# Two edits around the start of the second layer: where the first batch's last filter sums lie, and the order of the weights' sums on GpSimd

## The chip, the cores and the metric

The kernel runs on one core of a Trainium2 chip. The metric is the device time of one execution in microseconds (us). Lower is better. The engines are called as in the profile: PE (TensorE) does matmuls and PEld is its weight load; DVE is VectorE, ACT is ScalarE, POOL is GpSimd and SP is SyncE, which here only issues DMAs. Each engine takes its instructions strictly in the order in which the program emits them for it; a "queue" below is this order.

## The reference

A batch of 8 sequences (3008 positions, 256 channels) is filtered along the positions in the Fourier domain, and the result goes through a two-layer network with a hard-swish between the layers.

```python
X = np.fft.rfft(x, axis=1)                      # x: (8, 3008, 256)
Y = X * (filt_r + 1j * filt_i)[None]            # (1505, 256) filters
y = np.fft.irfft(Y, n=3008, axis=1).reshape(24064, 256)
h = y @ moe_w_in                                # (256, 2048)
g = h * np.clip(h + 3.0, 0.0, 6.0) / 6.0
out = g @ moe_w_out                             # (2048, 256)
```

## The kernel before

The Fourier transform is done by matmuls with tables, since 3008 is 47 times 64: a first stage (`a_unit`, or `a0_unit` for batch 0), a second (`b_unit`), the product with the filter (`f_unit` makes products, `y_unit` the sums of products, lines 454 to 461), and two inverse stages (`bi_unit`, `n_unit`) with trips through DRAM between them (`z_tmp`, `g_tmp`). For batch 0 all of this runs first, in the first 67 us; the batches 1 to 7 are threaded into the network's steps.

The network runs over 47 blocks of 512 tokens and, in each, over 8 pairs `p` of 128 hidden columns (256 columns a pair), so there are 8 steps to a block. Block 0 is done plainly (`plain_up`, `plain_down`: four products of 128 by 512 each way). From block 1 on, which is step 8, a Strassen-like scheme with seven products replaces eight (`up_1` to `up_5`, `g_sums`, `down`). It needs sums of weights beside the weights. The tile `w_all` has, for each pair and each of the two matrices, seven slots of 128 columns; the slots 0 to 3 take the raw weights and are read by the plain steps. `w_sums(i, late)` makes the sums for matrix `i % 2` of pair `i // 2` on GpSimd: with `late` false, three sums into the slots 4, 5 and 6, which read slots 0 to 3; with `late` true, one sum that overwrites slot 1, and so has to come after the plain step of that pair. That is 8 operations a pair, 64 in all. `up_1` of a pair needs the slot 0 and then slot 4 (`S1`) of its input matrix.

The weights come as 64-bit floats and are converted on DVE: `w_conv(i)`, seven instructions (lines 275 to 293) that turn the loaded words into slots 0 to 3 of a matrix; a pair is two conversions. The conversions 0 to 3 are done during batch 0, the other twelve in the steps 0 to 6 by `convert_one`: one in step 0, two in each of the steps 1 to 5, and number 15, the last, in step 6. A conversion's last instruction is at line 293. The load of the words of conversion `i + 2` goes out on SP's queue when the buffer of `i` is free.

The order is written out by hand: `plan` holds what is to be emitted at each step, and `at(step, fn, ...)` appends to it. In a plain step the order is `plain_up(p)`, then the step's early units (matmul stages, among them `bi_unit`), then `plain_down(p - 1)`, then the rest in the order of the `at` calls (conversions, sums of weights, stores, loads). Inside `plain_up`, `relu(i)` (line 615, ACT) reads the matmul's result from PSUM into a buffer `r`, and `hswish` (line 620, DVE) multiplies, and frees the PSUM tile.

Buffers come from rotating pools: a new tile takes the place of the oldest of its tag and waits for that one's readers. The tag `r` of the pool `rp` has two; it is used by a zero tile at the start, by the `y` tiles of batch 0, and by every `relu`. The pool `t1p` has two buffers of the tag `t1`; in batch 0 they take the results of `bi_unit(0, 0)`, `(0, 4)` and `(0, 8)`, which `g_store` writes to DRAM from GpSimd's queue, and afterwards the first stage's results of the later batches. The `y` tiles that matter here are those of `y_unit(0, 10)` and `y_unit(0, 11)`: they are read by `direct` (line 545) and, in step 0, by `bi_unit(0, 10)` (line 471).

`t_sums(k)` (line 563), four differences of the tokens of block `k`, is also on GpSimd's queue, between sums of weights.

Of the kernel before, what the change touches and what calls it, by code (L numbers as in the profile page):

```python
# [10 lines left out]
FP32 = mybir.dt.float32  # L11
# [20 lines left out]
P = 128  # L32
D = 256
# [12 lines left out]
NP = DFF // 256  # L46
# [90 lines left out]
def kernel(  # L137
# [25 lines left out]
    def pool(name, bufs, **kw):  # L163
        return ctx.enter_context(tc.tile_pool(name=name, bufs=bufs, **kw))

    const = pool("const", 1)
    t1p = pool("t1p", 2)
    t2p = pool("t2p", TB)
    sp = pool("sp", 2)
    yp = pool("yp", 3)  # L170
    t3p = pool("t3p", T3B)
    xtp = pool("xtp", 2)
    rp = pool("rp", 2)
# [21 lines left out]
    st = {}  # L195
# [257 lines left out]

    def y_unit(b, i):
        s1, s2 = st["y", b, i]
        y = yp.tile([P, 2, D], FP32, name="y") if b else rp.tile([P, 512], FP32, name="r", tag="r").rearrange(
            "p (u d) -> p u d", u=2)
        re, im = slice(0, HALF), slice(HALF, P)
        nc.vector.tensor_tensor(out=y[re], in0=s1[re], in1=s1[im], op=ALU.subtract)
        nc.vector.tensor_tensor(out=y[im], in0=s2[re], in1=s2[im], op=ALU.add)  # L460
        st["y", b, i] = y
# [271 lines left out]
    def at(step, fn, *a):  # L733
        plan.setdefault((step, fn in EARLY), []).append((fn, a))

    with tc.manual_schedule():
# [66 lines left out]
        for c in range(NT):  # L803
            for i in (2 * c, 2 * c + 1):
                b_unit(0, i)
                f_unit(0, i)
                if c == NT - 1:
                    y_unit(0, i)
            if c + 1 < NT:
                turn(c + 1)  # L810
            if c:
                bi_unit(0, 2 * c - 2)
                (g0_first if c == NT - 1 else lambda i: g_store(0, i))(2 * c - 2)
            if c == 4:
                t4_load(0, 0, KH - 3 * TC, 1)
# [22 lines left out]

        for i, s in enumerate((0, 1, 1, 2, 2, 3, 3, 4, 4, 5, 5, 6)):
            at(s, convert_one)  # L840
        for p in range(NP):
            for i in range(2):
                for late in range(2):
                    at(p + 6, w_sums, 2 * p + i, late)

        at(0, wai_load)
        at(2, x_load, 1, 2)
# [42 lines left out]
        for n in range(1, B):  # L890
            a_at, f_at, y_at, bi_at = places(n)
            for c, s in enumerate(a_at):
                at(s, a_unit, n, c)
                if n > 1:
                    at(s, a_sums, n, c)
                at(s, z_store, n, c, nc.sync if n == 1 else nc.gpsimd)
                if c >= 3:
                    at(max(a_at[c - 3], s - 6), x_load, n, c)
                elif n > 1:
                    at(max(prev[c + NB - 3], s - 6), x_load, n, c)  # L900
            for c in range(NT):
                s = f_at[2 * (c - TB) + (n == 1)] + 1 if c >= TB else a_at[-1] + 1
                at(s, t2_load, n, c)
                s = f_at[2 * (c - FB) + 1] + 1 if c >= FB else a_at[-1 if n > 1 else 3] + 1
                at(s, table_load, n, c)
            for i in range(NU):
                if i % 2 == 0 or n == 1:
                    at(f_at[i], b_unit, n, i)
                if i % 2 == 0:
                    at(bi_at[i // 2], bi_unit, n, i)  # L910
                    at(bi_at[i // 2], g_store, n, i)
                at(y_at[i], y_unit, n, i)
            for i in range(NU):
                at(f_at[i], f_unit, n, i)
            prev = a_at
# [4 lines left out]
        for i in range(len(items) + 1):  # L920
            up = i < len(items)
            k, p = items[min(i, len(items) - 1)]
# [92 lines left out]
```

## Time and profile before

| | |
|---|---|
| time, median of 6 runs | 2708.59 us (2706.83 to 2712.05) |
| the profiled execution: its own time | 2708.02 us |
| its span, first to last instruction | 2706.2 us |
| mean granted TensorE clock | 0.998 of full speed |
| PE, DVE, ACT, POOL busy | 2676.8, 2023.9, 1307.9, 373.4 us |
| `plain_up` of pairs 0 to 7: PE begins at | 67.13, 73.39, 80.39, 88.49, 98.40, 109.30, 120.72, 132.17 us |
| step 8 (`up_1` of block 1, pair 0): PE begins at | 142.08 us |
| sums of weights on POOL | 40 from 106.33 us, 24 from 173.21 us |

The times inside the execution count from the start of the span. A timeline line gives the start, the length, engine and line, the operation, output and inputs with their shapes and the count; in brackets stands the idle time of the engine before it and what ended that. Several instructions of one kind are merged into one line. A window line gives, for each engine, its busy time and the number of its instructions in that stretch, then the granted clock of PE, the busy share of the DMA engines and GB/s.

### The profile page before, as it was taken

The numbers are of one execution on the slowest core, as the hardware profiler recorded it, in microseconds if no ns is written. First come the engines' busy times: TensorE is split into PE (matmuls) and PEld (weight loads), VectorE is DVE, ScalarE is ACT, GpSimd is POOL, SyncE is SP. The second block draws the span as 40 slices with busy tenths as digits, with TensorE's granted clock in tenths as the row PEclk, the third lists the DMA queues.
The fourth block names the chain that finished last, engine by engine and source line by source line (L and its number), as shares of the span: only waits on it lengthen the run. The fifth ranks groups of instructions, "written<-read, shape, count | busy, mean of one in ns | idle before, by whom it ended". The sixth has DMA issues, their size and how long they took to land.

```text
span 2706.2 us, 48891 instructions
## 1 busy us (share of the span) xinstructions
PE 2676.8 (99%) x18846; PEld 2366.4 (87%) x18846; DVE 2023.9 (75%) x3503; ACT 1307.9 (48%) x2614; POOL 373.4 (14%) x598
## 2 busy tenths in 40 slices
PE   9899999999999999999999999999999999999998
PEld 6588888888988889888888888988888888899997
DVE  7958867787678876777767877678776778766665
ACT  3344444444544544444444545445454454444443
POOL 2421111100120011200121011210112111000000
PEclk9999999999999999999999999999999999999999
DMA  8732123211232113321133111331113311110000
GB/s 240 205 100 68 49 81 103 73 32 44 80 106 71 35 40 90 104 63 35 46 97 97 55 38 50 92 96 55 38 54 89 96 58 36 42 31 17 18 9 17
DMA packets 106598, 185.89 MB, mean 69 GB/s; under 512 B 23609, under 2 KB 66297, under 8 KB 106049
## 3 DMA queue, kind: packets, MB, share of 16 engines
q1 hardware_dynamic: 88607, 138.05, 18.2%
q0 software_dynamic: 17152, 44.22, 6.2%
q8 instruction: 149, 2.44, 0.4%
q14 instruction: 84, 0.69, 0.1%
q10 hardware_dynamic: 606, 0.49, 0.1%
HBM read 110.74 MB, written 71.93 MB: 67 GB/s over the span
## 4 chain that ended last, share of the span: by engine, by line
PE 95%; DVE 2%; DMA 1%; SPq 0%; issue 0%; ACT 0%; POOL 0%; POOLq 0%; DVEq 0%
PE po L646 43%; PE al L570 24%; PE be L570 17%; PE psn L524 4%; PE psf L471 2%; PE psf L385 2%; PE psf L428 1%; PE po L352 1%; PE po L437 0%; DMA xs<-in_x_dram 0%; PE psf L437 0%; DVE g L620 0%; PE al L779 0%; DVE y L277 0%; DVE y L288 0%
## 5 line engine op out<-in xcount | busy, mean ns | idle before, releaser
L646 PEld LDWEIGHTS po<-w_all,g 128*128 128x128 f32 x10304 | 1363.1, 191 | 149.5 <-issue 41.4
L646 PE MATMUL po<-w_all,g 128*128 128x128 f32 x10304 | 1403.3, 276 | 0.6 <-DVE g L620 0.6
L615 ACT ACTIVATE r<-h,half_c 128x512 f32<-128x512 f32 x736 | 531.3, 722 | 329.4 <-DVE h L596 317.4
L620 DVE SCALAR_TENSOR_TENSOR g<-r,h 128x512 f32<-128x512 f32 x736 | 507.6, 690 | 206.6 <-ACT r L615 192.2
L570 PE MATMUL al<-xt,w_all 128*128 128x256 f32 x2208 | 660.1, 381 | 1.1 <-DVE h L601 0.6
L570 PE MATMUL be<-xn,w_all 128*128 128x256 f32 x1472 | 437.8, 379 | 0.0
L596 DVE TENSOR_TENSOR h<-be,s 128x512 f32<-128x512 f32 x368 | 254.3, 691 | 222.0 <-PE be L570 209.9
L570 PEld LDWEIGHTS al<-xt,w_all 128*128 128x128 f32 x2208 | 335.3, 192 | 2.5 <-issue 1.3
L570 PEld LDWEIGHTS be<-xn,w_all 128*128 128x128 f32 x1472 | 279.7, 190 | 37.9
L610 ACT ACTIVATE h<-al 128x256 f32<-128x256 f32 x368 | 141.4, 384 | 343.2 <-PE al L570 343.2
L601 DVE TENSOR_TENSOR h<-al,s 128x256 f32<-128x256 f32 x368 | 156.2, 425 | 166.0 <-PE al L570 164.8
L628 DVE TENSOR_TENSOR g<-g 128x512 f32<-128x512 f32 x368 | 255.9, 695 | 12.7
L591 ACT ACTIVATE s<-al 128x256 f32<-128x256 f32 x368 | 141.4, 384 | 205.4 <-PE al L570 203.3
L582 ACT ACTIVATE s<-be 128x256 f32<-128x256 f32 x368 | 141.4, 384 | 176.3 <-PE be L570 176.3
L570 PE MATMUL al<-xn,w_all 128*128 128x256 f32 x736 | 219.9, 381 | 0.5 <-ACT h L610 0.5
L570 PE MATMUL be<-xt,w_all 128*128 128x256 f32 x736 | 218.9, 379 | 0.0
L630 DVE TENSOR_TENSOR g<-g 128x256 f32<-128x256 f32 x368 | 169.9, 462 | 12.5
L581 ACT ACTIVATE s<-al 128x256 f32<-128x256 f32 x368 | 141.4, 384 | 70.9 <-PE al L570 70.8
L627 DVE TENSOR_TENSOR g<-g 128x256 f32<-128x256 f32 x368 | 157.0, 427 | 12.6
L570 PEld LDWEIGHTS be<-xt,w_all 128*128 128x128 f32 x736 | 139.8, 190 | 18.9
L402 POOL DMA_DIRECT2D z_tmp<-t x192 | 95.2, 502 | 417.5 <-DVE t L395 399.1
L563 POOL TENSOR_TENSOR xt<-xn 128x256 f32<-128x256 f32 x92 | 68.7, 747 | 473.8 <-ACT xn L530 453.5
(139 smaller groups left out, 1810.4 us busy)
## 6 DMA issues: line engine op xcount, KB each, us to landing
g_tmp<-t POOLq DMA_DIRECT2D x96, 256.0 KB, 3.7
t<-g_tmp SPq DMA_DIRECT2D x188, 120.0 KB
t<-z_tmp SPq DMA_DIRECT2D x42, 512.0 KB
z_tmp<-t POOLq DMA_DIRECT2D x192, 96.0 KB, 3.4
out_dram<-o SPq DMA_DIRECT2D x321, 47.0 KB
xs<-in_x_dram SPq DMA_DIRECT2D x112, 128.0 KB
ft<-in_filt_r_dram SPq DMA_DIRECT2D x168, 64.0 KB
ft<-in_filt_i_dram SPq DMA_DIRECT2D x168, 64.0 KB
```

What stands on the lines that cost most here:

```text
L570: nc.tensor.matmul(ps, w_in[p][:, w, :], x, start=start, stop=stop, skip_group_check=True)
L581: nc.scalar.activation(out=s[:, 0, :], in_=al, func=AXT.Copy)
L582: nc.scalar.activation(out=s5, in_=be[:, 1, :], func=AXT.Copy)
L591: nc.scalar.activation(out=s[:, 1, :], in_=al, func=AXT.Copy)
L596: nc.vector.tensor_tensor(out=st["h"][0].rearrange("p (a n) -> p a n", a=2), in0=be, in1=s, op=ALU.add)
L601: nc.vector.tensor_tensor(out=st["h"][1][:, 256:512], in0=al, in1=s5, op=ALU.add)
L615: nc.scalar.activation(out=r, in_=st["h"][i], func=AXT.Relu, bias=half_c, scale=1.0 / 6.0)
L620: nc.vector.scalar_tensor_tensor(out=st["g", k, p][:, o:o + 2, :].rearrange("p a n -> p (a n)"), in0=st["r", i], scalar=1.0, in1=st["h"][i ...
L627: v.tensor_tensor(out=g[:, G1, :], in0=g[:, G3, :], in1=g[:, G22, :], op=ALU.add)
L628: v.tensor_tensor(out=g[:, G3:G2 + 1:2, :], in0=g[:, G3:G1 + 1, :], in1=g[:, G11:G11 + 1, :].broadcast_to([P, 2, 256]), op=ALU.subtract)
L630: v.tensor_tensor(out=g[:, G4, :], in0=g[:, G12, :], in1=g[:, G2, :], op=ALU.subtract)
L646: nc.tensor.matmul(st["po", k][bank][:, part, u, :], g[:, a, ts(u, P)], w_out[p][:, w, :], start=(p == 0 and n in OPENS and u == 0), stop= ...
```

## The change

In the first hunk, the two `y` tiles of batch 0 take the two halves of one `t1` buffer instead of two `r` buffers. `y_unit(0, 10)` takes the buffer that `bi_unit(0, 0)` had, and `bi_unit(0, 8)`, which comes right behind, now takes the one that `bi_unit(0, 4)` had, not that of `bi_unit(0, 0)`.

In the second hunk, the six sums of pair 7 that don't overwrite raw weights (`w_sums(14)` and `w_sums(15)` with `late` false) go from step 13 to step 6, ahead of the sums of pair 0. The two late sums of pair 7 stay in step 13. The order on GpSimd's queue from step 6 on is then: six of pair 7, eight each of the pairs 0 to 4, `t_sums(2)`, eight each of the pairs 5 and 6, two of pair 7. Before it was eight each of the pairs 0 to 4, `t_sums(2)`, eight each of the pairs 5 to 7. The six sums read what the conversions 14 and 15 write.

```diff
     def y_unit(b, i):
         s1, s2 = st["y", b, i]
-        y = yp.tile([P, 2, D], FP32, name="y") if b else rp.tile([P, 512], FP32, name="r", tag="r").rearrange(
-            "p (u d) -> p u d", u=2)
+        if b == 0 and i % 2 == 0:
+            st["y0"] = t1p.tile([P, 2, 2, D], FP32, name="t1")
+        y = yp.tile([P, 2, D], FP32, name="y") if b else st["y0"][:, i % 2, :, :]
...
         for i, s in enumerate((0, 1, 1, 2, 2, 3, 3, 4, 4, 5, 5, 6)):
             at(s, convert_one)
+
+        for i in range(2):
+            at(6, w_sums, 2 * NP - 2 + i, False)
         for p in range(NP):
             for i in range(2):
-                for late in range(2):
-                    at(p + 6, w_sums, 2 * p + i, late)
+                if p < NP - 1:
+                    at(p + 6, w_sums, 2 * p + i, False)
+                at(p + 6, w_sums, 2 * p + i, True)
```

## The prediction

> **What bounds the kernel now.** I read the page first (engines, then the chain that ended last), then the timelines of PE, ACT, DVE and POOL from 66 to 190 us, where the edited lines run, and last the granted clock in small windows.
>
> ```profile
> PE 2676.8 (99%) x18846; PEld 2366.4 (87%) x18846; DVE 2023.9 (75%) x3503; ACT 1307.9 (48%) x2614; POOL 373.4 (14%) x598
> PE 95%; DVE 2%; DMA 1%; SPq 0%; issue 0%; ACT 0%; POOL 0%; POOLq 0%; DVEq 0%
> ```
>
> PE bounds the whole: its waits between 140 and 420 us, batch 1's stages included, are 1.6 us in all. A gain must come out of the 29 us in which PE is idle or out of matmuls that run slow, and what PE saves before 142 us lasts to the end, since all that follows is paced by PE. The waits that PE's timeline shows in the plain steps:
>
> ```profile
> 70.77 1.09 PE L471 MATMUL psf<-r,wi 64*64 64x512 f32 x8
> 73.39 1.98 PE L657 MATMUL al<-xn,w_all 128*128 128x512 f32 x4 [1.54 <-DVE g L620]
> ...
> 109.30 1.98 PE L657 MATMUL al<-xn,w_all 128*128 128x512 f32 x4 [0.82 <-DVE g L620]
> 120.72 1.98 PE L657 MATMUL al<-xn,w_all 128*128 128x512 f32 x4 [3.04 <-DVE g L620]
> 122.54 1.88 PE L657 MATMUL be<-xn,w_all 128*128 128x512 f32 x4
> 132.17 3.24 PE L657 MATMUL al<-xn,w_all 128*128 128x512 f32 x4 [3.08 <-DVE g L620]
> 135.20 2.36 PE L657 MATMUL be<-xn,w_all 128*128 128x512 f32 x4
> ```
>
> Four waits for DVE's hard-swish, 8.5 us, and after the last of them the same four matmuls take 3.24 instead of 1.98 us. The window of the granted clock (first value after the POOL count) says why:
>
> ```profile
> 133.00:134.00 1.00, 1.00 (x2) 0.34 (x1) 0.93 (x3) 0.00 (x0) 0.92 (x2) 0.50 0.80 168
> ```
>
> Half speed, from about 132.7 to 136.6 us. What DVE does before those waits, in a conversion at 89 us and in one at 115 us, and POOL:
>
> ```profile
> 89.24 0.75 DVE L277 SCALAR_TENSOR_TENSOR y<-bits,top_c,y 128x512 int32<-128x512 int32 x1
> 90.02 0.43 DVE L279 TENSOR_SCALAR y<-y 128x512 int32<-128x512 int32 x1
> 90.37 0.42 DVE L281 TENSOR_SCALAR bits<-bits 128x512 int32<-128x512 int32 x1
> ...
> 115.46 0.83 DVE L277 SCALAR_TENSOR_TENSOR y<-bits,top_c,y 128x512 int32<-128x512 int32 x1
> 116.32 0.56 DVE L279 TENSOR_SCALAR y<-y 128x512 int32<-128x512 int32 x1
> 116.81 0.68 DVE L281 TENSOR_SCALAR bits<-bits 128x512 int32<-128x512 int32 x1
> ```
>
> ```profile
> 106.33 28.48 POOL L299 TENSOR_TENSOR w_all<-w_all 128x128 f32<-128x128 f32 x40
> 169.96 0.73 POOL L563 TENSOR_TENSOR xt<-xn 128x256 f32<-128x256 f32 x1 [35.15 <-ACT xn L530]
> 173.21 14.38 POOL L299 TENSOR_TENSOR w_all<-w_all 128x128 f32<-128x128 f32 x24
> ```
>
> DVE has no idle time from 74 to 130 us and every conversion instruction is longer while POOL runs its 40 sums (106.33 to 134.81 us); at 135.14 us line 288 is back at 0.69 from 0.83. So in the plain steps 4 to 7 DVE is the bound, stretched by POOL's sums, which nobody needs before step 8.
>
> **First hunk: the buffer.** ACT's `relu` of pair 0 starts at 71.93 us after 4.14 us idle, put down to PE's line 471, `bi_unit(0, 10)`: that reads the `y` tiles, whose `r` buffers `relu` wants. With `y` elsewhere `relu` needs only its matmul. Pair 1 shows that latency: 73.39 to 75.42, so 67.13 + 2.03 = 69.16 us. The second: 75.22 to 77.13, so 68.95 + 1.91 = 70.86 us, and its hard-swish 0.74 later (72.52 to 73.26), 71.60 instead of 73.26. DVE is free of conversion 3 at 70.12 us, so conversion 4 starts 1.66 us earlier; its words landed by 66 us. PE goes on at 71.86 us, the end of line 471, instead of 73.39: 1.53 us.
>
> The added wait: `bi_unit(0, 8)` now writes the buffer of `bi_unit(0, 4)`, whose two stores left POOL at 45.5 and 46.0 us and took 5.6 and 6.1 us to land, so 52.1 us; ACT's copy (line 474) starts at 52.20. Behind it on ACT are the stores of `g0_first`, for which `t4_load`, `n_first` and pair 0 wait, so lateness is paid in full. Store landings of this line lie between 2.9 and 7.4 us, so the cost is 0 to 1.3; I take 0.2, by the row of this very store. `y_unit(0, 10)` itself waits for stores of 36 us, long landed. The two halves of one tile are tracked by region: at 153.77 us PE reads one slot of `g` while line 630 still writes another (to 154.3). Net: DVE 1.45 us earlier.
>
> **Second hunk: the order on POOL.** After `t_sums(1)` POOL now meets the sums of pair 7, which need conversion 14 (ends 131.51 us before) and 15 (137.35). So the stretch with the 40 sums beside the conversions 10 to 15 becomes idle. The time from one pair's first hard-swish on DVE to the next, with two conversions between, is 9.55 us without POOL (78.04 to 87.59), and was 11.10, 11.42 and 11.45 us for the steps that follow 97.47, 108.57 and 119.99. Saved: 1.87 and 1.90 in the last two; of the 1.55 in the first most is `t_sums(1)` (103.8 to 106.3), which stays: I take 0.45 (bounds 0.2 and 1.5). Sum 4.2 us. PE's own work per step is 8.37 us (109.30 to 117.67) against 9.55, so DVE stays the bound and the gain is PE's: with 1.45 before it, `plain_up` of pair 7 starts 5.7 us earlier, at 126.5 us, after waits of about 0.4, 1.1 and 1.2 us.
>
> Clock: the four matmuls each of `al` and `be` took 3.03 and 2.30 us to the next start against 1.82 and 1.81 in pair 6, so the drop cost 1.70 us. The drop followed the second idle time of 3 us in the trace (3.04, then 3.08); the new ones are at most 1.3. I count 1.70 as gained, bounds 0 and 1.70. [...]
>
> What becomes late: the sums of pair 0 are now behind conversion 15. It ends about 131.4 us; three sums of pair 7's output matrix, then S1, at 0.60 each (14.38 / 24, beside the network's DVE work) give 133.9 us. PE wants S1 at 142.51 - 5.7 - 1.7 = 135.1; at 126.5 us plus 3.6, 1.0 and 3.5 us of its own work and 0.43, the same. So no wait, with 1.2 us to spare. Pair by pair POOL needs 4.8 us and PE's steps are 7.0 to 8.4, so the slack grows; `t_sums(2)` comes at 163 us and POOL is through its 43 sums at about 157. Steps 8 to 11 get POOL's company on DVE: at 177 to 186 us it stretched lines 627, 628 and 630 by 0.14 each and PE had no gap there. I take 0.2 us for the switch at step 8. [...] The loads stay hidden: words come 3.9 to 5.0 us after their issue (at line 288 of two conversions before), and DVE then has 6.9 us of other work.
>
> **The sum.** 1.45 + 4.2 + 1.7 - 0.2 = 7.2 us off the profiled execution's 2708.02 (span 2706.2 plus 1.8 around it): 2700.8. The median of the runs stands 0.57 above that execution, so 2701.3.
>
> **Rivals.** (1) Partial gain: the clock still drops, or the new bound on DVE is a load (slack 1.9 to 2.3 us, with the same bytes in 5 us less), and 1.7 to 4 us of the 7.2 are lost: about 2704. For it: DMA engines are 0.8 to 0.9 busy in several windows there. Against: no DVE wait for words now. (2) The second hunk gives nothing, as the conversions are stretched by DMA traffic, not POOL: first hunk alone, 2708.6 - 1.4 = 2707. Against: the stretch ends with POOL's last sum at 134.8 while the DMA share stays at 0.8. (3) Slower: the sums of weights come late in block 1. In series from 131.5 us, S1 of pair 4 is the 36th sum; at d us each it is there at 131.5 + 36 d, and PE wants it at 175.92 - 7.4 = 168.5. Up to d = 1.03 nothing is paid; at 1.23 the whole 7.2 is gone, and at 1.4 the time is 2708.6 + 6 = 2715. For it: single sums took up to 1.01. Against: means 0.60 and 0.71.
>
> **Chances.** Forecast 64%, (1) 21%, (2) 8%, (3) 7%. The forecast's own span: 0.2 to 1.5 in the first DVE step, 0 to 1.3 for the store and 0.5 us of spread of medians give 2699 to 2702.8. The range 2698.5 to 2706 takes in (1). A measurement of this kernel tells 0.2%, 5.4 us, from no change: 2703.2 is the edge of faster. The forecast and a little of (1) are faster, 0.66; the rest of (1), and (2), the same, 0.27; slower 0.07.
>
> **What the profile after would show.** `relu` of pair 0 near 69.2 us with its idle before it ended by `al`; six sums on POOL at about 125 and 131 us, then 40 in one run; line 281 at 0.43 and line 277 at 0.75 in conversions 11 to 14; `plain_up` of pair 7 at 126.5 us and step 8 at 134.7; clock 1.00 throughout 120 to 140. Wrong if ACT's line 474 waits beyond 53 us, if PE at line 570 waits for POOL's line 299, or if DVE shows idle time before line 275.

## The result, and the profile after

The changed kernel takes 2700.88 us (median of 15 runs, 2700.09 to 2705.59) against 2708.58 (33 runs of the kernel before): a ratio of 0.9973, 95% interval 0.9966 to 0.9980. The forecast was 2701.3.

The execution that was profiled first is not a typical one: its own time is 2704.62 us (span 2702.8), 3.7 above the median. Its lines, in the order of those shown of before. The page's engines and the chain that ended last:

```profile
PE 2679.4 (99%) x18846; PEld 2368.8 (88%) x18846; DVE 2021.1 (75%) x3503; ACT 1308.0 (48%) x2614; POOL 365.6 (14%) x598
PE 94%; DVE 3%; DMA 1%; SPq 1%; issue 0%; ACT 0%; POOL 0%; POOLq 0%; DVEq 0%; ACTq 0%
```

PE's timeline (line numbers are one higher than before from line 458 on):

```profile
68.96 3.78 PE L658 MATMUL al<-xn,w_all 128*128 128x512 f32 x4
...
75.84 1.99 PE L658 MATMUL al<-xn,w_all 128*128 128x512 f32 x4
...
111.48 1.98 PE L658 MATMUL al<-xn,w_all 128*128 128x512 f32 x4 [0.55 <-DVE g L621]
121.03 1.98 PE L658 MATMUL al<-xn,w_all 128*128 128x512 f32 x4 [1.17 <-DVE g L621]
130.67 1.98 PE L658 MATMUL al<-xn,w_all 128*128 128x512 f32 x4 [1.27 <-DVE g L621]
132.49 1.88 PE L658 MATMUL be<-xn,w_all 128*128 128x512 f32 x4
```

The gap before pair 1 is gone, the gaps of 0.82, 3.04 and 3.08 us are 0.55, 1.17 and 1.27, and the matmuls of pair 7 run at full speed (1.82 us from `al` to `be`). But those of pair 0 now take 3.78 us. The window of the granted clock shows that the half-speed stretch is now here, from 66.7 to 73.5 us:

```profile
70.00:71.00 1.00, 1.00 (x3) 0.48 (x2) 0.90 (x2) 0.00 (x0) 0.00 (x0) 0.50 1.04 395
```

DVE in conversion 11, and POOL:

```profile
112.40 0.75 DVE L277 SCALAR_TENSOR_TENSOR y<-bits,top_c,y 128x512 int32<-128x512 int32 x1
113.19 0.43 DVE L279 TENSOR_SCALAR y<-y 128x512 int32<-128x512 int32 x1
113.53 0.42 DVE L281 TENSOR_SCALAR bits<-bits 128x512 int32<-128x512 int32 x1
```

```profile
130.15 1.71 POOL L299 TENSOR_TENSOR w_all<-w_all 128x128 f32<-128x128 f32 x3 [21.39 <-issue]
135.60 23.12 POOL L299 TENSOR_TENSOR w_all<-w_all 128x128 f32<-128x128 f32 x43 [3.74 <-DVE w_all L293]
...
170.00 10.14 POOL L299 TENSOR_TENSOR w_all<-w_all 128x128 f32<-128x128 f32 x18
```

The conversions beside which POOL is now idle are back at 0.75, 0.43 and 0.42 us. POOL waits 21 us for conversion 14 (the line names no releaser, but that conversion ends at 130.01) and 3.7 us for 15, and is through with its 43 sums 8 us before `t_sums(2)` can start.

Comparing this one execution with the one of before gives 3.4 us of span, less than half of what the runs show. So the first thing that I wanted was the same kernel once more.

### The profile page after: what moved, and what is told of

Read it like the earlier page. It is cut to its first block, busy times and chain, and to the rows that moved or that the text cites. A ratio compares the mean times of both kernels' runs of the same rounds, so it can differ in the third digit from the quotient of the medians.

```text
span 2702.8 us, 48891 instructions
## 1 busy us (share of the span) xinstructions
PE 2679.4 (99%) x18846; PEld 2368.8 (88%) x18846; DVE 2021.1 (75%) x3503; ACT 1308.0 (48%) x2614; POOL 365.6 (14%) x598
## 3 DMA queue, kind: packets, MB, share of 16 engines
q8 instruction: 149, 2.44, 0.4%
## 4 chain that ended last, share of the span: by engine, by line
PE 94%; DVE 3%; DMA 1%; SPq 1%; issue 0%; ACT 0%; POOL 0%; POOLq 0%; DVEq 0%; ACTq 0%
PE po L647 43%; PE al L571 23%; PE be L571 17%; PE psn L525 4%; PE psf L472 2%; PE psf L385 2%; PE psf L428 1%; PE po L352 1%; DMA t<-g_tmp 0%; PE psf L437 0%; SPq L724 0%; DMA out_dram<-o 0%; PE po L437 0%; PE al L780 0%; DVE g L621 0%
## 5 line engine op out<-in xcount | busy, mean ns | idle before, releaser
L492 POOL DMA_DIRECT2D g_tmp<-t x84 | 52.7, 632 | 584.4 <-ACT t L475 584.4
```

## The experiments

**The changed kernel again, and each hunk alone.** The two diffs are the hunks shown above.

> The changed kernel once more, for an execution whose clock does not drop early. Theory (the prediction's terms): 2700.9 us; plain_up of pair 7 about 5.6 us earlier than before when both are counted from line 437's last matmuls, ACT's first relu about 2.0 us after the start of plain_up's first matmul, PE gaps of 0.5, 1.2 and 1.3 us before pairs 5, 6 and 7, clock 1.00 from 60 to 140 us. Rival (the drop at 66 to 73 us in the profiled execution belongs to the change): it is there again and most runs are near 2704.6.

> First hunk alone. Theory: DVE 1.5 to 1.7 us earlier from pair 0 on, the gaps of 3 us before pairs 6 and 7 unchanged, so 2708.6 - 1.5 = 2707.1 us. Rival (nothing, because the store of bi_unit(0, 4) is waited for, or because the hard-swish waits for something else): 2708.6.

> Second hunk alone. Theory: 3.9 us from the DVE intervals after pairs 3, 4 and 5 and, in the executions that dropped, 1.7 us of clock: 2708.6 - 5.6 = 2703.0 us, and 0 us of POOL waits on PE. Rival (the two hunks only gain together): 2706 or more.

Measured: `both` 2701.02 us (6 runs), ratio 0.9974 (0.9963 to 0.9986); `buffer_only` 2705.43 (11 runs), 0.9993 (0.9984 to 1.0002); `order_only` 2703.18 (11 runs), 0.9981 (0.9972 to 0.9989); the kernel before, measured beside them, 2707.81 (22 runs). The interval of `buffer_only` takes in 1, but six of its eleven runs, 2704.47 to 2705.43, lie below the lowest of all 107 runs of the kernel before, 2706.37.

ACT's timeline of `both` shows the first hunk's work (`relu` of pair 0, both halves):

```profile
69.44 0.69 ACT L616 ACTIVATE r<-al,half_c 128x512 f32<-128x512 f32 x1 [1.37 <-PE al L658]
71.16 0.69 ACT L616 ACTIVATE r<-be,half_c 128x512 f32<-128x512 f32 x1 [1.03 <-PE be L658]
```

Both wait only for their matmuls, the first 2.02 us after `al` begins (67.42). In `both` the second hard-swish of pair 0 comes 4.46 us after `al` begins, 6.13 before the change: 1.67 us. From there to `plain_up` of pair 7 it is 54.99 us, 58.91 before: 3.92. The clock of pair 7's matmuls is 1.70. DVE's first hard-swish of the pairs 3 to 6, before and in `both`, and PE at pair 7 and at step 8 in `both`:

```profile
97.47 0.68 DVE L620 SCALAR_TENSOR_TENSOR g<-r,al 128x512 f32<-128x512 f32 x1
108.57 0.68 DVE L620 SCALAR_TENSOR_TENSOR g<-r,al 128x512 f32<-128x512 f32 x1
119.99 0.67 DVE L620 SCALAR_TENSOR_TENSOR g<-r,al 128x512 f32<-128x512 f32 x1
131.44 0.68 DVE L620 SCALAR_TENSOR_TENSOR g<-r,al 128x512 f32<-128x512 f32 x1
```

```profile
96.08 0.68 DVE L621 SCALAR_TENSOR_TENSOR g<-r,al 128x512 f32<-128x512 f32 x1
106.97 0.68 DVE L621 SCALAR_TENSOR_TENSOR g<-r,al 128x512 f32<-128x512 f32 x1
116.50 0.68 DVE L621 SCALAR_TENSOR_TENSOR g<-r,al 128x512 f32<-128x512 f32 x1
126.13 0.68 DVE L621 SCALAR_TENSOR_TENSOR g<-r,al 128x512 f32<-128x512 f32 x1
```

```profile
126.87 1.98 PE L658 MATMUL al<-xn,w_all 128*128 128x512 f32 x4 [1.26 <-DVE g L621]
...
135.08 0.59 PE L571 MATMUL al<-xn,w_all 128*128 128x256 f32 x2
```

The intervals are 11.10, 11.42 and 11.45 us before and 10.89, 9.53 and 9.63 in `both`. In all, from `al` of pair 0 to step 8 it is 67.66 us (67.42 to 135.08), 74.95 before (67.13 to 142.08): 7.29 less. What is left of the 7.6 us between the spans (2698.6 and 2706.2) is small: `al` of pair 0 starts 0.29 later, step 8 to the last matmuls takes 2549.54 instead of 2549.64, and the tail after them 13.98 instead of 14.48. The stretch from step 8 to the last matmuls stays between 2549.5 and 2550.0 us in the profiles of before, the changed kernel, each hunk alone and the kernels below that leave step 8 as it is. What is saved ahead of step 8 stays saved.

`buffer_only` keeps POOL's 40 sums where they were, and with them the long gaps and the drop of the clock (0.72 granted from 130 to 135 us):

```profile
119.88 1.98 PE L658 MATMUL al<-xn,w_all 128*128 128x512 f32 x4 [3.05 <-DVE g L621]
...
131.34 3.00 PE L658 MATMUL al<-xn,w_all 128*128 128x512 f32 x4 [3.08 <-DVE g L621]
```

So the hunks add up, as both theories of them say (2.4 and 4.6 us alone by the medians, 6.8 together): the first takes away a wait of ACT, the second the stretching of the conversions. Neither needs the other.

**What stretches the conversions.** Into the stretch that the change made idle I put other work for GpSimd, sums of the same size in one kernel, memsets in the other; the results are overwritten.

```diff
+        def dummy_sums(n):
+            w = w_in[NP - 1]
+            for i in range(n):
+                nc.gpsimd.tensor_tensor(out=w[:, 4, :], in0=w_in[0][:, 0, :], in1=w_in[0][:, 2, :], op=ALU.add)
+        at(4, dummy_sums, 30)      # fill_sums;  fill_sets: 50 times nc.gpsimd.memset(w[:, 4:7, :], 0.0)
```

> The changed kernel with 30 further sums of the same size on GpSimd behind t_sums(1), in the stretch that the change made idle; their result is overwritten. Theory (POOL's work beside the conversions is what stretched them): 30 x 0.71 = 21 us beside conversions 10 to 14, DVE's intervals back at about 11.1, 11.4 and 11.4 us, 3.9 us lost and, where the clock drops again, 1.7 more: 2704.8 to 2706.5. Rival (the transfers stretched them, or the order itself matters): 2700.9.

> The same, but with 50 memsets of 128 x 384 on GpSimd, which write and read nothing, about 0.33 to 0.45 us each by the 32 x 1024 memset's 0.94 us, some 20 us in all. Theory (any POOL work on SBUF stretches the conversions): as with sums, 2704.8. Rival (only POOL's reads collide with DVE's second input): lines 277, 288, 290 and 293 stay at 0.75 and 0.69 us, at most lines 275, 279 and 281 grow, and the time is 2700.9 to 2702.

Measured: `fill_sums` 2704.55 us (11 runs; ratio 0.9986, 0.9977 to 0.9995), `fill_sets` 2704.04 (11 runs; 0.9984, 0.9976 to 0.9993). The sums give back 3.6 us of the gain, with no transfer added and the order of what is needed unchanged. The groups of DVE instructions by shape (busy time, mean ns), from conversions 11 to 14 or most of them, first with sums, then with memsets:

```profile
L277 DVE SCALAR_TENSOR_TENSOR y<-bits,top_c,y 128x512 int32<-128x512 int32 x4 | 3.3, 825 | 0.1
L281 DVE TENSOR_SCALAR bits<-bits 128x512 int32<-128x512 int32 x3 | 2.0, 680 | 0.0
L279 DVE TENSOR_SCALAR y<-y 128x512 int32<-128x512 int32 x3 | 1.7, 562 | 0.1
```

```profile
L279 DVE TENSOR_SCALAR y<-y 128x512 int32<-128x512 int32 x4 | 3.1, 766 | 0.1
L277 DVE SCALAR_TENSOR_TENSOR y<-bits,top_c,y 128x512 int32<-128x512 int32 x4 | 3.0, 752 | 0.1
L281 DVE TENSOR_SCALAR bits<-bits 128x512 int32<-128x512 int32 x4 | 2.9, 717 | 0.0
```

Sums bring all of them back to the lengths of before (825, 680 and 562 ns). Memsets leave line 277, with two inputs in SBUF, at 752 ns (and the lines 288, 290 and 293 at 692 to 693), and hit only instructions with one input: 766 and 717 ns instead of 427 and 422 for lines 279 and 281, and a little line 275 (473 instead of 418). So it is POOL's work, and the kind of work decides which of DVE's instructions it hits. For the memsets neither expectation holds whole: which lines grow is as the rival says, but the time is near the theory's: the lines with one input alone lengthen DVE's intervals from 9.53 and 9.63 us to 10.82 and 11.13. That answers the prediction's second rival (the transfers) with no.

**How late the sums may be.** Eight further sums between those of pair 7 and those of pair 0.

```diff
         for i in range(2):
             at(6, w_sums, 2 * NP - 2 + i, False)
+        at(6, dummy_sums, 8)       # into the slot that pair 0's first sum writes next
```

> The changed kernel with 8 further sums between those of pair 7 and those of pair 0 (they write the slot that pair 0's first real sum then writes). Theory (S1 has 1.2 to 1.5 us to spare, and from there PE pays in full): 8 x 0.55 = 4.4 us, PE waits about 3 us for POOL at step 8's second product, 2703.9 us. Rival (no wait since PE does not need S1 then): 2700.9.

Measured: 2705.59 us (11 runs, 2703.47 to 2708.46; ratio 0.9988, 0.9979 to 0.9997). PE's timeline at step 8:

```profile
137.58 0.70 PE L571 MATMUL be<-xt,w_all 128*128 128x256 f32 x2 [2.38 <-POOL w_all L299]
```

The eight sums took 4.19 us and PE waited 2.38, so 1.8 us were to spare: the third rival's mechanism is there, its place as named, and the change stays that far from it. The cost is more than the wait, 4.7 us by the medians: in the profiled execution, the fastest of the eleven, the clock then ran at half speed from 139.0 to 142.4 us. What made the other ten longer still isn't shown.

**The drops of the clock.** The 107 runs of the kernel before (a 108th, of 5426.76 us, is left out) fall into three groups: 52 below 2708 us (median 2707.2), 27 from 2708 to 2709.9 (2708.7) and 28 above (2710.7). A drop at pair 7 costs 1.70 us in the profile, one at pair 0 some 2.9 (in the first execution after the change, 10.77 us from `n_first` to pair 1's `al`, 7.9 in `both`). I took the two upper groups for executions with a drop, and tried that on the kernel before, with nothing but idle matmuls added in PE's gaps.

```diff
+        fill = psU.tile([P, 512], FP32, name="al")            # ahead of n_first: keep_clock2 only
+        nc.tensor.matmul(fill, wi[:, 0:2, :].rearrange("p a m -> p (a m)"),
+                         st["y", 0, NU - 1].rearrange("p u d -> p (u d)"), start=True, stop=True)
...
+                if p in (5, 6):                               # end of steps 5 and 6: both
+                    fill = psO.tile([P, 2, 2, P], FP32, name="po2").rearrange("p a u m -> p (a u m)")
+                    for n in range(2):
+                        nc.tensor.matmul(fill, wf[:, 0:2, :].rearrange("p a m -> p (a m)"), wa[:, 0:512],
+                                         start=True, stop=True)
```

> The kernel before with two idle 512-column matmuls (1.7 us) at the end of steps 5 and 6, in PE's two gaps of 3 us; neither hunk is in it. Theory (the gaps of 3 us let the clock drop in part of the executions): DVE unchanged, gaps of about 1.3 us, clock 1.00 from 120 to 140 us; 1.7 us less where it dropped, and the runs near 2708.6 move to 2707.0. Rival (the gaps have nothing to do with the clock): the times spread as before, 2708.6.

> keep_clock with one more idle 512-column matmul (0.86 us) in PE's gap of about 1.3 us ahead of n_first, near 63 us. Theory (that gap is what lets the clock drop at 66 to 73 us, in part of the executions, 3.7 us each): all runs at 2706.6 to 2707.5, none near 2710.7. Rival (the drop has another cause, or the added matmul delays n_first): about a third of the runs near 2710.7, or all of them 0.5 to 1 us later.

Measured: `keep_clock` 2707.23 us (11 runs): seven from 2706.61 to 2707.28, one at 2709.28, three from 2710.40 to 2711.75. `keep_clock2` 2707.38 us: all eleven from 2706.41 to 2708.28. The ratios to before, 0.9998 (0.9990 to 1.0007) and 0.9996 (0.9987 to 1.0005), cannot tell a difference. The groups say a little: with the first fill one run of eleven lies in the middle group, with both fills none in the upper. At the shares of before so few come by chance about once in five and once in thirty.

The mean granted clock of each run says more. It is on record for 74 of the 107 runs of before, and none of them has 0.999; nor has any of the 22 of `buffer_only` and `fill_sums`, which have gaps of 3 us too; of the 22 runs with fills ten have, and of the changed kernel's 18 fastest fourteen. (A single 0.998 tells nothing: the profile of `order_only` has it with the clock at 1.00 from 50 to 150 us, and the clock also falls in the tail: in the profile of before it is 0.98 from 2690 to 2700 us and 0.50 from 2700 us on.) So, as an estimate from these means, there are drops in more runs than the two upper groups, and the low group of before (0.998 in 30 runs, 0.997 in 9) can hardly be free of them, as I had taken it to be; it does not pay for them. The middle group has 0.998 in all its 16, the upper 0.997 or 0.996 in 18 of 19. No profile shows a run of the low group. But one of `fill_sums` shows a drop that costs nothing, at pair 6:

```profile
123.57 2.42 PE L658 MATMUL al<-xn,w_all 128*128 128x512 f32 x4 [3.18 <-DVE g L621]
...
134.62 1.98 PE L658 MATMUL al<-xn,w_all 128*128 128x512 f32 x4 [0.98 <-DVE g L621]
```

The four matmuls from 123.57 on take 2.42 us instead of 1.98, the granted clock is 0.50 from 125 to 128 us, and PE still waits 0.98 us for DVE ahead of pair 7. Most likely the low group has its drop there.

In `keep_clock` the timeline shows pair 7 at full speed behind a gap of 1.4 us (granted clock 1.00 from 130 to 145 us):

```profile
133.02 1.98 PE L657 MATMUL al<-xn,w_all 128*128 128x512 f32 x4 [1.37 <-DVE g L620]
```

So, by the groups, the kernel before has two places where a drop of the clock costs time, each in about a quarter of its runs. The change takes the one at pair 7: of 21 runs of the changed kernel 18 lie from 2700.09 to 2701.52 and three from 2704.62 to 2705.98, which is the group with the drop at pair 0. That this group is rarer than before (3 of 21 against 28 of 107) can be chance: so few come about once in six.

**A faster version.** What `t_sums(1)` costs DVE in the intervals before pairs 3 and 4 (9.88 and 10.89 us in `both`, against 9.55) was left. `lead14` lets only the sums that need conversion 14 lead; `lead14_tsums` also moves `t_sums(1)` behind them; `lead14_warm` adds the idle matmul ahead of `n_first`.

```diff
-        if dh and (t + n) // BLK > t // BLK > 0:               # in n_unit: lead14_tsums
+        if dh and (t + n) // BLK > t // BLK > 1:
...
-        for i in range(2):
-            at(6, w_sums, 2 * NP - 2 + i, False)
+        at(6, w_sums, 2 * NP - 2, False)
+        at(6, t_sums, 1)                                       # lead14_tsums
...
-                if p < NP - 1:
+                if (p, i) != (NP - 1, 0):
```

> A version that may beat the changed one: only the three sums that need conversion 14 lead (those that need 15 go back to step 13) and t_sums(1) moves behind them, so that POOL does nothing beside conversions 9 to 14. Theory (DVE's two-conversion interval is the bound until pair 7): the intervals before pairs 3 and 4 become 9.55 us instead of 9.89 and 10.88, 1.7 us less, 2699.2 us; conversion 15 is stretched by about 0.9 us, off the path. Rival (PE's own work of 9.91 us in the steps with n_unit is the bound there): 0.5 us less at most, 2700.4. Second rival: S1 or xt of block 1 late at step 8: PE waits there, no gain.

> Between the changed kernel and lead14_tsums: only the three sums that need conversion 14 lead, t_sums(1) stays where it was. Theory (waiting for conversion 15 as well is neither a gain nor a loss, and lead14_tsums gained by t_sums alone): 2700.9 us, DVE intervals as in the changed kernel up to pair 7, and S1 earlier. Rival (the earlier start of pair 0's sums is worth something at step 8): 2699 to 2700.

> lead14_tsums with the same idle matmul ahead of n_first. Theory: all runs at 2698.0 to 2699.3, none near 2702.3. Rival: as without it, or 0.5 us later.

Measured: `lead14_tsums` 2698.72 us (5 runs, 2698.05 to 2702.26; ratio 0.9966, 0.9954 to 0.9979), 2.3 us below `both`, measured beside it. PE's timeline:

```profile
106.34 1.88 PE L658 MATMUL al<-xn,w_all 128*128 128x512 f32 x4
...
114.93 1.98 PE L658 MATMUL al<-xn,w_all 128*128 128x512 f32 x4 [0.32 <-DVE g L621]
...
124.57 1.98 PE L658 MATMUL al<-xn,w_all 128*128 128x512 f32 x4 [1.26 <-DVE g L621]
```

Pair 5 no longer waits. DVE's intervals are 9.53 to 9.63 us up to pair 6, and 7.27 instead of 5.44 us with conversion 15, which now has POOL beside it and delays nobody. From `al` of pair 0 to step 8 it is 66.01 us, 1.65 less than in `both`, as expected. PE's own work did become the bound at pair 5, as the rival says, but only there: DVE is late again at pairs 6 and 7, and so the whole step of DVE counts.

`lead14` is inconclusive: 2702.74 us (10 runs; 0.9979, 0.9970 to 0.9989): four from 2700.39 to 2701.03, as expected, three near 2702.8 and three near 2704.4. The profiled execution (2701.03) shows the intervals of the changed kernel and no drop. The three near 2704.4 have a mean clock of 0.997, as the changed kernel's runs with a drop at pair 0; those near 2702.8 have 0.998 and 0.999, as the fast ones, so the clock is not what makes them longer, and what does is open. `lead14_warm` has 2699.47 us (5 runs, 2698.96 to 2700.50; 0.9968, 0.9956 to 0.9981): no run near 2702, but not faster than `lead14_tsums`.

## Why the prediction was right, and where it was not

The forecast, 7.2 us off the profiled execution and 2701.3 for the median, was right, and right by its steps; two of them were mis-sized and one was counted too simply. That it came within 0.5 us of the median is in part luck. It counted the 1.70 us of the clock in full, which only a group of the runs pays, and the runs that do not pay it gained 6.3 us where the other terms say 5.5. And 2708.58, the median of before here, lies in the group with the drop at pair 7; over all 107 runs the median is 2708.06.

- **The buffer.** 1.66 us for DVE was predicted, 1.67 measured in `both`. The 0.2 for the added wait was not there: in the first execution after the change the two stores landed at 52.2 and 52.9 us, and ACT's copy started at 53.29, released by PE, as before. The prediction had named a start beyond 53 us as a sign that it is wrong. The sign was met to the letter, but not in its meaning: all work there lay about 1 us later, and ACT's idle time ahead of the copy was 2.38 us, 2.34 before; in `both` the copy started at 52.75. By the medians of the fastest groups the hunk is worth 2.1 us (2707.2 to 2705.0), a little more than the profile accounts for.
- **POOL's order.** 4.2 predicted, 3.92 measured. The part that was too large is the interval before pair 4, 0.45 predicted and 0.21 measured (10.89 instead of 11.10): even more of its excess belongs to `t_sums(1)`. The two others were 1.89 and 1.82, predicted 1.87 and 1.90. By the fastest groups: 4.1 us (2707.2 to 2703.1). The 0.2 for the switch at step 8 was not there either (2549.54 us from there to the last matmuls, 2549.64 before).
- **The clock.** 1.70 predicted and measured between two profiles (half speed was from 132.75 to 136.16 us, somewhat shorter than the prediction read). But only a group of the executions of before pays for a drop at pair 7. Most of the median's gain is the other two terms: between the fastest groups, which do not pay for one, it is 6.3 us (2707.2 to 2700.9), and 7.7 between the medians, since the median of before lies in the group that has the drop at pair 7. A single profile could not show that; the six times of before, spread over 5 us, could have warned me.
- **Short gaps and the clock.** The 1.70 was counted in full because the new gaps, at most 1.3 us, are shorter than the two of before, 3.04 and 3.08. That gaps so short are safe was my estimate; no run shows it in general. Ahead of the pairs 5 to 7 it held in the first execution after the change: behind 0.55, 1.17 and 1.27 us the granted clock stayed at 1.00. But in the same execution PE was idle for 1.39 us ahead of `n_first`, and half speed followed from 66.7 us on. The prediction's line "clock 1.00 throughout" looked only at 120 to 140 us.
- **What becomes late.** S1 of pair 0 had 1.2 us to spare in the prediction, 1.8 by `late8`. No wait of PE for POOL in any profile without added sums.
- **The rivals.** The partial gain and the transfers: no DVE wait for words in the plain steps of any profile. The late sums: real, but 1.8 us away. The range's upper part was there for an execution like the one profiled first, though for another reason than the one given.

About 0.7 us between the fastest groups' 6.3 and the 5.6 of the two terms are left. The tail after the last matmuls begin has most of it: 14.5 us in the three profiles with neither hunk, 14.2 and 14.3 with one, 13.9 to 14.0 in the eight with both. Why it is shorter no run shows.

## What to carry to other kernels

Where one engine's work stretches another's, look at whether the stretched one is the bound in that stage, and at when the stretching work is really wanted: here the first of 40 operations ran 36 us too early because nothing held them back, and a dependent operation put ahead of them in the queue was enough to shift them (POOL idle for 21.39 us ahead of it, with 40 sums behind it). Take the price of such company from the same instruction with and without it (line 279: 0.56 us beside POOL's sums, 0.43 without). Before adding up a gain from one profile, look at how the run times group: a cost that only some executions pay (here a drop of the clock behind a gap) counts as far as the median has it.

## What the runs showed of the hardware

In the profiles the granted clock fell to 0.50 behind gaps of very different length, and not always: at pairs 6 and 7 and step 8 behind gaps of 3.18 us (`fill_sums`), 3.08 (before, `buffer_only`), 2.75 (`fill_sets`) and 2.38 (`late8`), and not behind 3.04 in before, 3.05 in `buffer_only` or 2.44 in `fill_sets`; ahead of `n_first` behind 1.39 (the changed kernel) and 1.59 (`fill_sums`), and not behind 1.75 in `buffer_only`.

It then stayed at half for 3.4 us in five of these seven drops (3.41 in before) and for 6.8 in the two behind the gap ahead of `n_first` (66.67 to 73.49 in the changed kernel). No run shows what decides whether a gap is followed by a drop, or how long the drop lasts.

With idle matmuls in all the gaps, none of eleven runs lay in the upper group (`keep_clock2`), and six of them have a mean clock of 0.999.

What a DVE instruction lost beside POOL's work depended on the kind of both. Line 277, with two inputs in SBUF, took 752 ns in `both`, where POOL is idle, 752 beside the memsets of `fill_sets` and 825 beside the sums of `fill_sums`. Line 279, with one input, took 427, 766 and 562 ns. Beside sums of 0.71 us each (28.48 us for 40 in before) the instructions with two inputs lost 0.07 to 0.14 us (0.75 to 0.83 at line 277, 0.69 to 0.83 at line 288), and at most 0.41 (line 288, 1.10) beside an operation of `t_sums` of 0.91. No run shows why.
